# Gates turned on chip and stored as rows, in a gated mix of local attention and a Mish MLP

## The chip, the cores and the metric

The kernel runs on one core of a Trainium2 chip. The core has five engines with queues of their own: TensorE (PE in the profile) for matrix products, VectorE (DVE), ScalarE (ACT) and GpSimd (POOL) for everything between them, and SyncE (SP), which here only issues DMAs. Each works through its queue in order and waits on semaphores where it needs another's result. DMAs move data between the device's memory and the on-chip memory, which has 128 partitions. The metric is device time in microseconds; less is better.

## The reference

From one input x of 2048 rows and 640 columns two branches are computed: local attention with 32 heads, in which each position looks at 8 earlier positions, 2 apart, and an MLP with a Mish between its two products. A gate for each row mixes the two.

```python
def reference(A_x, A_wqkv, A_wo, B_x, B_w1, B_b1, B_w2, gate_w):
    ...
    x = A_x
    g = _sigmoid((x * gate_w).sum(-1, keepdims=True))
    a = _A_ref(x, A_wqkv, A_wo)
    b = _B_ref(x, B_w1, B_b1, B_w2)
    return g * a + (1 - g) * b
```

The change touches only how 1 - g, one number for each of the 2048 rows, gets from where it is computed to where it is used.

## The kernel before, in words

The rows are worked on in two halves (P = 0 and 1) of 1024, each as 8 slots of 128 rows. Products are made of float32 operands split into a high and a low part, three matmuls for one product (`mm3`, L457 to L462). The splitting is done by ACT (the high part, L410) and by DVE or POOL (the low part, L413); most loads land in `raw` or `hb` buffers and are split into `pair` buffers.

The work in order of TensorE's queue: for each half and each quarter of the heads a unit `qkv` (L634) makes queries, keys and values into PSUM banks `qb` and `sb`, from which ACT copies them (L624 to L630). Between the units lie the first product of the MLP (class `Quad`, L883, with sums and differences of blocks in the manner of Strassen) and Mish (ACT, L732 and L918), whose results go through `hb` buffers, are summed by `combined` (L804, run at L808) and stored to memory as `act` and `actt` blocks. Then come the second product of the MLP (`mlp2`, L1146) and the output product of the attention (`wo_part`, L1312). Attention itself (L497) runs on DVE: multiply (L517), sum (L520), softmax (L538 to L549), weigh (L558) and sum (L562), then a turn in blocks of 32 x 32 (L473) and four stores to `o`. Sums of the second-layer weights (`sums_of`, L983, with L998 and L1011) are made along the way and stored as `s`.

Each weight block of the first unit of a half (hq = 0) carries `gate_w` as extra columns. After a slot's product, ACT copies the one column of row sums into `zt[:, P, s]` (L630): 128 partitions by 8 slots. `make_gates` (L694) turns them into gates: ACT takes exp(-z) (L700), DVE adds 1, takes the reciprocal (g, used by the attention's softmax at L548) and computes 1 - g into `gc` (L696 to L698). One DMA (L702) then stores `gc` to `g_d[P]`, which lies in memory as 8 rows of 128 floats: slot by row. Element by element that is a transpose: consecutive floats of a partition of `gc` go to places 512 bytes apart. Much later `gates_in` (L1150) reads four rows at a time, broadcast over 128 partitions, into a buffer by which the MLP's results are multiplied (`gated`, L1173).

Nothing is placed in the engines' queues by hand. Each piece of work is a task (engine, estimated ns, function, what it comes after, buffers), and `Plan.run` (L105) simulates the engines with these estimates and emits the tasks in the order in which the simulation starts them. A task may be given to "ANY", and then goes to POOL, or to DVE when it is due. Among ready tasks the lowest rank goes first; `rank=2.0` for the store of the gates is behind nearly all other work of SP. The `size` of a DMA task sets how long the simulation lets it hold the wire: size/330 ns (L91), after all that is on the wire already (L200 to L203). So an estimate, a rank or a size changes the order of all later work. Buffers of a kind form a ring with a fixed number (6 `hb`, 8 `raw`, 24 `pair`), which are handed out in order.

Of the kernel before, what the change touches and what calls it, by code (L numbers as in the profile page):

```python
# [8 lines left out]
F32 = mybir.dt.float32  # L9
F32R = mybir.dt.float32r  # L10
AF = mybir.ActivationFunctionType
OP = mybir.AluOpType
# [54 lines left out]
class Plan:  # L67
# [21 lines left out]
    def add(self, eng, ns, fn, after=(), rank=0.0, take=(), hold=(), size=0, kind="", late=0):  # L89
        t = Task(eng, ns, fn, rank, size / 330.0)  # L90
        t.kind, t.late, t.near, t.patience = kind, late, self.NEAR, self.PATIENCE  # L91
        if eng == "POOL" and type(ns) is not tuple:
            t.ns = (ns, ns)
        for p in after:
            if p is not None:
                p.then.append(t)
                t.waits += 1
        t.take = list(take)
        t.hold = list(take) + [b for b in hold if b not in take]
        for b in t.hold:  # L100
            b.left += 1
        self.tasks.append(t)
        return t
# [136 lines left out]
def kernel(ctx: ExitStack, tc: tile.TileContext, x, wq, wo, w1, b1, w2, out):  # L240
    nc = tc.nc
    scale = DH ** -0.5
    V, G, A = nc.vector, nc.gpsimd, nc.scalar

    keep = ctx.enter_context(tc.tile_pool(name="keep", bufs=1))
# [93 lines left out]
    add = plan.add  # L339

    SOON, NEXT, LATER, LAST = 0.0, 1.0, 2.0, 3.0
# [5 lines left out]
    bound = keep.tile([1, HQ, 7], F32)  # L347
    zt = keep.tile([128, 2, 8], F32)
    gate = keep.tile([128, 2, 8], F32)
    gc = keep.tile([128, 2, 8], F32)  # L350
    hx = keep.tile([128, 2, 8, NQ, RQ], F32)

    keep.tile([128, 118], F32, name="gap")
# [11 lines left out]
    g_d = [dram.tile([8, 128], F32, name=f"g{P}") for P in range(2)]  # L365
# [5 lines left out]
    KV = [Late(lambda i=i: kvq[i][:, :15 * ROW].rearrange("p (s a f) -> p s a f", a=2, f=QF)) for i in range(3)]  # L371
# [27 lines left out]
    def consts_g():  # L399
        G.memset(KV[0][0:1, 0:7], 0.0)  # L400

        G.memset(bound, -BIG / scale)


    cg = [add("POOL", 2200, consts_g, rank=-1), add("DVE", 2200, lambda: V.memset(KV[1][0:1, 0:7], 0.0), rank=-3.0)]


    def split(raw, hi, lo, n, after, eng, hold, take=(), rank=SOON):
# [17 lines left out]
    def dma(out_ap, in_ap, after=(), rank=0.0, take=(), hold=(), size=262144, late=0):  # L426
        return add("SP", 450, lambda: nc.sync.dma_start(out_ap(), in_ap()), after, rank=rank, take=take, hold=hold, size=size, late=late)
# [206 lines left out]
    def qkv(u, P, hq, between={}):  # L634
# [51 lines left out]
        if not hq:  # L686
            gates[P] = [make_gates(P, [ev[i][2] for i in range(8)])]
# [3 lines left out]
    g_done = {}  # L691


    def make_gates(P, after):  # L694
        def run():
            V.tensor_scalar(zt[:, P], zt[:, P], 1e30, 1.0, op0=OP.min, op1=OP.add)  # L696
            V.reciprocal(gate[:, P], zt[:, P])
            V.tensor_scalar(gc[:, P], gate[:, P], -1.0, 1.0, op0=OP.mult, op1=OP.add)  # L698

        t = add("ACT", 200 + 2 * TABLE, lambda: A.activation(zt[:, P], zt[:, P], AF.Exp, scale=-1.0), after, rank=NEXT)  # L700
        t = add("DVE", 500, run, [t], rank=NEXT)
        g_done[P] = dma(lambda: g_d[P].rearrange("s p -> p s"), lambda: gc[:, P], [t], rank=2.0, size=400000)  # L702
        return t


# [572 lines left out]
    def rows(tb, kc):  # L1278
        return o_d[tb][kc * 128:(kc + 1) * 128]
# [419 lines left out]
```

## Time and profile before

| | us |
|---|---|
| median of 3 runs | 631.7 |
| lowest and highest run | 627.73, 631.99 |
| the profiled execution | 631.72 |
| its span, first to last instruction | 630.0 |

The table of the profile that says the most is the busy time of each engine in 40 equal slices of the span, in tenths, with TensorE's granted clock and the DMA engines' share:

```profile
PE   9999999999999999999999979999999999999997
PEld 7878888888888888888888758888888888888886
DVE  8699999999989999899999999999999989879955
ACT  6587637736476554624556365765845743556520
POOL 1487557657747553386564563586436750010000
PEclk9999999999999999999999989999999999999999
DMA  8668684577857799979987777668899664799613
```

A digit of 9 means 90% or more. Each slice is 15.75 us. A time in microseconds in the text below counts from the start of the span; a line such as L698 is that of the kernel before. Other views group instructions by line, follow the chain of waits back from the last instruction, or list engines in order of time, with the idle time before an instruction and what ended it in square brackets.

### The profile page before, as it was taken

The page shows a single profiled execution, that of the slowest core. Times are in us where ns is not written, and L with a number is a line of the kernel's source. Part 1 is how long each engine was busy: PE and PEld are TensorE (multiplying, and loading weights), DVE is VectorE, ACT ScalarE, POOL GpSimd, SP SyncE. Part 2 cuts the span into 40 slices and gives each one's busy share as a digit, 9 for nine tenths or more (in the row PEclk, how much of TensorE's full clock was granted, in tenths as well). Part 3 has the DMA queues.
Part 4 walks back from the last instruction along what each step waited for, and adds up shares of the span by engine and source line. Part 5 has one row for each costly group of instructions (what it writes and reads, how often), then busy time and mean ns, then how long its engine had stood idle before and what let it go on. Part 6 is the DMA issues. An engine that isn't in the chain of part 4 may idle for free.

```text
span 630.0 us, 9053 instructions
## 1 busy us (share of the span) xinstructions
PE 619.8 (98%) x2743; PEld 514.4 (82%) x2743; DVE 581.3 (92%) x547; ACT 349.9 (56%) x790; POOL 306.8 (49%) x281
## 2 busy tenths in 40 slices
PE   9999999999999999999999979999999999999997
PEld 7878888888888888888888758888888888888886
DVE  8699999999989999899999999999999989879955
ACT  6587637736476554624556365765845743556520
POOL 1487557657747553386564563586436750010000
PEclk9999999999999999999999989999999999999999
DMA  8668684577857799979987777668899664799613
GB/s 322 193 196 124 227 285 113 185 231 240 270 176 205 229 183 222 287 195 306 280 235 253 218 248 237 176 190 242 255 252 307 189 212 151 218 305 358 230 50 117
DMA packets 99552, 140.36 MB, mean 223 GB/s; under 512 B 13152, under 2 KB 53344, under 8 KB 99280
## 3 DMA queue, kind: packets, MB, share of 16 engines
q1 hardware_dynamic: 96144, 134.02, 68.0%
q0 software_dynamic: 3072, 5.51, 6.0%
q8 instruction: 21, 0.34, 0.2%
q10 hardware_dynamic: 288, 0.26, 0.1%
q14 instruction: 27, 0.22, 0.1%
HBM read 87.78 MB, written 51.00 MB: 220 GB/s over the span
## 4 chain that ended last, share of the span: by engine, by line
PE 74%; DVE 9%; DMA 8%; POOL 4%; issue 3%; ACT 2%; SPq 0%; DVEq 0%; POOLq 0%; ACTq 0%
PE qb L460 15%; PE qb L461 15%; PE qb L462 15%; PE sb L462 9%; PE sb L460 9%; PE sb L461 9%; DMA ot<-o 2%; DVE lg L520 2%; DVE pr L517 2%; POOL hb L808 2%; DVE pr L558 2%; DMA s<-raw 1%; DMA raw<-in_w 1%; POOL pair L413 1%; DMA ot<-ot 1%
## 5 line engine op out<-in xcount | busy, mean ns | idle before, releaser
L413 POOL TENSOR_TENSOR pair<-raw,pair 128x512 fp32r<-128x512 f32 (+3 forms) x132 | 163.6, 1274 | 102.5 <-ACT pair L410 50.7
L460 PE MATMUL qb<-pair 128*128 128x512 f32 (+1 forms) x467 | 181.8, 389 | 5.3 <-ACT hb L732 4.4
L461 PE MATMUL qb<-pair 128*128 128x512 f32 (+1 forms) x467 | 181.3, 388 | 0.0
L462 PE MATMUL qb<-pair 128*128 128x512 f32 (+1 forms) x467 | 181.3, 388 | 0.0
L410 ACT ACTIVATE pair<-raw 128x512 fp32r<-128x512 f32 (+3 forms) x223 | 129.5, 609 | 85.2 <-DMA raw<-actt 24.4
L460 PE MATMUL sb<-pair 128*128 128x512 f32 (+1 forms) x294 | 113.7, 387 | 0.0
L462 PE MATMUL sb<-pair 128*128 128x512 f32 (+1 forms) x294 | 113.7, 387 | 0.0
L461 PE MATMUL sb<-pair 128*128 128x512 f32 (+1 forms) x294 | 113.7, 387 | 0.0
L460 PEld LDWEIGHTS qb<-pair 128*128 128x128 f32 x467 | 87.9, 188 | 24.1 <-ACT hb L732 5.3
L462 PEld LDWEIGHTS qb<-pair 128*128 128x128 f32 x467 | 88.1, 189 | 17.4
L461 PEld LDWEIGHTS qb<-pair 128*128 128x128 f32 x467 | 88.1, 189 | 17.1
L558 DVE TENSOR_TENSOR pr<-kvq,pg 128x1280 f32<-128x1280 f32 x64 | 93.3, 1485 | 1.0
L517 DVE TENSOR_TENSOR pr<-kvq,qg 128x2560 f32<-128x2560 f32 x32 | 90.0, 2812 | 1.6
L520 DVE TENSOR_REDUCE lg<-pr 128x128 f32<-128x2560 f32 x32 | 90.2, 2818 | 0.8
L562 DVE TENSOR_REDUCE kvq<-pr 128x320 f32<-128x2560 f32 x32 | 90.2, 2817 | 0.8
L413 DVE TENSOR_TENSOR pair<-raw,pair 128x512 fp32r<-128x512 f32 (+3 forms) x91 | 65.5, 743 | 10.7 <-ACT pair L410 10.6
L462 PEld LDWEIGHTS sb<-pair 128*128 128x128 f32 x294 | 55.2, 188 | 11.3
L460 PEld LDWEIGHTS sb<-pair 128*128 128x128 f32 x294 | 55.2, 188 | 11.3
L461 PEld LDWEIGHTS sb<-pair 128*128 128x128 f32 x294 | 55.2, 188 | 11.2
L808 POOL TENSOR_TENSOR hb<-hb 128x512 f32<-128x512 f32 x41 | 53.5, 1313 | 18.1 <-DVE lg L539 4.7
L624 ACT ACTIVATE kvq<-qb 128x320 f32<-128x320 f32 x63 | 27.3, 434 | 57.2 <-PE qb L462 56.8
L410 ACT ACTIVATE pair<-hb 128x512 fp32r<-128x512 f32 (+3 forms) x62 | 36.6, 590 | 2.8 <-PE qb L462 1.4
(156 smaller groups left out, 735.0 us busy)
## 6 DMA issues: line engine op xcount, KB each, us to landing
actt<-hb SPq DMA_DIRECT2D x52, 256.0 KB, 3.3
raw<-in_w SPq DMA_DIRECT2D x40, 256.0 KB, 4.1
act<-hb SPq DMA_DIRECT2D x38, 256.0 KB, 3.0
raw<-actt SPq DMA_DIRECT2D x37, 256.0 KB, 4.1
raw<-in_wq SPq DMA_DIRECT2D x30, 248.0 KB, 3.5
raw<-act SPq DMA_DIRECT2D x29, 256.0 KB, 3.6
raw<-in_x SPq DMA_DIRECT2D x23, 256.0 KB, 3.5
o<-ot SPq DMA_DIRECT2D x64, 80.0 KB, 3.0
```

What stands on the lines that cost most here:

```text
L410: a = add("ACT", act_ns(n), lambda: A.activation(hi(), raw(), AF.Copy), after, rank=rank, take=take, hold=hold)
L413: return (V if e == "DVE" else G).tensor_tensor(lo(), raw(), hi().bitcast(F32), op=OP.subtract)
L460: nc.tensor.matmul(ps, ah, bh, start=first, stop=False, skip_group_check=more)
L461: nc.tensor.matmul(ps, ah, bl, start=False, stop=False, skip_group_check=more)
L462: nc.tensor.matmul(ps, al, bh, start=False, stop=last, skip_group_check=more)
L517: return V.tensor_tensor(pr, window(kv, s0, 0), qg[:, :, None, :].to_broadcast([128, 2, W, QF]), op=OP.mult)
L520: V.tensor_reduce(lg_w[:, s0:s0 + 2], pr.rearrange("p s w (h d) -> p s w h d", d=DH), op=OP.add, axis=AX.X)
L558: V.tensor_tensor(pairs[:, s].rearrange("p k i (h d) -> p k i h d", d=DH), vw, pg[:, s0 + s].rearrange("p (k i) h -> p k i h", i=2)[:, :, ...
L562: V.tensor_reduce(q[:, s0:s0 + 2], pairs.rearrange("p s k i f -> p s f k i"), op=OP.add, axis=AX.XY)
L624: a = add("ACT", 330, lambda: A.activation(kv[:, 7 + s], ps.t[:, QF:3 * QF].rearrange("p (a b) -> p a b", a=2), AF.Copy), [done] + before, ...
L808: return (V if e == "DVE" else G).tensor_tensor(t.t[:, i:i + n], a.t[:, j:j + n], b.t[:, k:k + n], op=op)
```

## The change

`gc` grows from 8 to 32 columns for each half and is filled with zeros at the start; the gates go into its first 8 columns. DVE turns each block of 32 partitions by 32 columns (`V.transpose`) into a second tile `gt`, in which slot s of a block of 32 rows now lies in partition 32 i + s. SP then issues four stores for each half, each of 8 partitions by 32 floats: 8 pieces of 128 bytes. The estimates that the planner is given change with it: 2200 to 2300 ns on POOL, 500 to 700 on DVE, 450 to 1800 on SP, and a size of 400000 to 65536.

```diff
-    gc = keep.tile([128, 2, 8], F32)
+    gc = keep.tile([128, 2, 32], F32)
+    gt = keep.tile([128, 2, 32], F32)
...
+        G.memset(gc, 0.0)
...
-    cg = [add("POOL", 2200, consts_g, rank=-1), add("DVE", 2200, lambda: V.memset(KV[1][0:1, 0:7], 0.0), rank=-3.0)]
+    cg = [add("POOL", 2300, consts_g, rank=-1), add("DVE", 2200, lambda: V.memset(KV[1][0:1, 0:7], 0.0), rank=-3.0)]
...
-            V.tensor_scalar(gc[:, P], gate[:, P], -1.0, 1.0, op0=OP.mult, op1=OP.add)
+            V.tensor_scalar(gc[:, P, :8], gate[:, P], -1.0, 1.0, op0=OP.mult, op1=OP.add)
+            V.transpose(gt[:, P], gc[:, P])
...
-        t = add("DVE", 500, run, [t], rank=NEXT)
-        g_done[P] = dma(lambda: g_d[P].rearrange("s p -> p s"), lambda: gc[:, P], [t], rank=2.0, size=400000)
+        t = add("DVE", 700, run, [t], rank=NEXT)
+
+        def rows():
+            for i in range(4):
+                nc.sync.dma_start(g_d[P][:, 32 * i:32 * (i + 1)], gt[32 * i:32 * i + 8, P])
+
+        g_done[P] = add("SP", 1800, rows, [t], rank=2.0, size=65536)
```

## The prediction

> **What bounds the kernel now.** I read the page first, then the busy time in equal stretches, then who waited for whom on PE.
>
> ```profile
> span 630.0 us, 9053 instructions
> PE 619.8 (98%) x2743; PEld 514.4 (82%) x2743; DVE 581.3 (92%) x547; ACT 349.9 (56%) x790; POOL 306.8 (49%) x281
> ```
> ```profile
> 40.00:50.00 10.00, 8.97 (x40) 7.11 (x39) 9.73 (x7) 8.64 (x18) 9.75 (x9) 1.00 0.82 187
> ...
> 360.00:370.00 10.00, 6.44 (x28) 4.75 (x26) 9.86 (x7) 7.87 (x16) 6.53 (x6) 1.00 0.72 236
> 370.00:380.00 10.00, 9.84 (x37) 8.13 (x38) 9.72 (x10) 4.22 (x14) 3.87 (x4) 0.83 0.95 285
> ```
> ```profile
> PE qb L460 <- ACT hb L732: 4.4, 2, 3.4
> PE qb L460 <- ACT hb L918: 0.8, 2, 0.5
> ```
>
> A stretch row gives the stretch, its length, then the busy time of PE, weight load, DVE, ACT and POOL, the granted clock, the DMA share and GB/s. PE is busy 619.8 of 630.0 us: a change can give back only PE's idle time and what slow clock follows it. Inside the work that is 1.0 us near 41, before any gate exists, and 4.2 us between 358 and 370 (in the waits, 3.4 of the 4.4 on L732 and the 0.8 on L918). The rest of the 10.2 us is the two ends of the program. So I look at the 358 to 370 stop and what feeds it.
>
> ```profile
> 358.41 0.69 ACT L918 ACTIVATE hb<-qb,bias 128x512 f32<-128x512 f32 x1 [10.00 <-DMA actt<-hb]
> ```
> ```profile
> 370.16 0.49 PE L460 MATMUL qb<-pair 128*128 128x496 f32 x1 [3.41 <-ACT hb L732]
> ```
> ```profile
> 42.55 0.23 PE qb L461
> ```
> ```profile
> 371.86 0.41 PE qb L460
> ...
> 374.34 0.41 PE qb L460
> 374.76 0.37 PE qb L461
> ```
>
> The last two fences are from the chain of waits: start, length, piece. The matmuls that follow the 3.41 us stop step at 0.41 us instead of 0.23 us, seven of them from 371.86 to 374.34 and one of 0.37: 7 x 0.18 + 0.14 = 1.4 us lost to the clock, which is the 0.83 in the 370 to 380 row. After the 1.03 us stop near 41 the step is 0.23 at once. The stop at 366 is therefore worth 3.41 + 1.4 = 4.8 us. ACT was late because a store had not freed its hb buffer; the store's source is written by DVE and POOL, and DVE is 98 to 99% busy through this stretch. DVE's lateness is what PE pays for here, so I ask where DVE lost time before 358.
>
> ```profile
> 247.26 0.42 DVE L538 TENSOR_REDUCE mx<-lg 128x32 f32<-128x256 f32 x1 [0.55 <-ACT lg L530]
> ```
> ```profile
> 267.68 0.42 DVE L998 TENSOR_TENSOR raw<-raw 128x256 f32<-128x256 f32 x1 [2.77 <-DMA raw<-in_w]
> ...
> 279.21 0.42 DVE L538 TENSOR_REDUCE mx<-lg 128x32 f32<-128x256 f32 x1 [1.07 <-ACT lg L530]
> ```
>
> Between the second gate (225 us) and 358, DVE waited 0.55 + 2.77 + 1.07 = 4.4 us, the largest part for a load.
>
> **What is removed.** The two old stores, in the view of their tile, and DMA traffic around them:
>
> ```profile
> L698 DVE TENSOR_SCALAR gc<-gate x2: 171/650/1128, 45.2 to 225.2; 128x8 f32<-128x8 f32 x2
> L427 SPq DMA_DIRECT2D g<-gc x2: 389/390/392, 46.3 to 228.8; - x2
> ```
> ```profile
> DMA to landing us min/median/max: 10.2/10.5/10.7
> ```
> ```profile
> 48.00:50.00 2.00, 2.00 (x11) 1.65 (x10) 1.91 (x2) 0.94 (x5) 2.00 (x2) 1.00 1.29 54
> ```
> ```profile
> 230.00:235.00 5.00, 5.00 (x24) 4.16 (x23) 4.86 (x6) 1.43 (x3) 3.91 (x5) 1.00 1.14 91
> 235.00:240.00 5.00, 5.00 (x25) 4.26 (x24) 4.86 (x4) 0.86 (x4) 4.49 (x4) 1.00 1.00 129
> ```
> ```profile
> DMA packets 99552, 140.36 MB, mean 223 GB/s; under 512 B 13152, under 2 KB 53344, under 8 KB 99280
> ```
> ```profile
> h<-pair SPq DMA_DIRECT2D x8, 32.0 KB, 2.8
> ```
>
> Each store moves 128 x 8 gates of 4 bytes, 4 KB, which by the shape of its destination are 1024 packets, and lands after about 10.45 us, where another small store lands after 2.8. Meanwhile the engines are full (shares of 1.29, 1.14, 1.00) and move almost nothing. From 230 to 240 they move about 110 GB/s against the mean of 223: 10 x 113/223 = 5 us of DMA work is pushed back; beside the first store the row from 48 to 50 shows 54 GB/s. An estimate per packet: (10.45 - 2.8) / (1024/16) = 0.12 us on each of 16 engines. The new stores have 4 x 8 = 32 packets of 128 bytes; at that price 0.24 us spread over 16, 3.8 us if one engine had them all. I take under 0.5 us.
>
> Who stood behind the second store:
>
> ```profile
> 228.31 9.38 DMA s<-raw
> ```
> ```profile
> 255.17 7.78 DMA ot<-o
> ```
> ```profile
> raw<-in_w SPq DMA_DIRECT2D x40, 256.0 KB, 4.1
> ot<-o SPq DMA_DIRECT2D x12, 256.0 KB, 4.0
> s<-raw SPq DMA_DIRECT2D x14, 64.0 KB, 3.8
> ```
>
> The store of sums issued at 228.31, just ahead of the gate store, took 9.38 us against a median of 3.8 and lies on the chain. The chain goes on through SP and a 7.78 us DMA at 255 (median 4.0), which finds the engines full with what was pushed back. The load that DVE waited for at 267.68 falls into the same crowd. I credit the change with that 2.77 us: between nothing (the crowd at 255 to 267 is also its own traffic) and 2.77 + 1.07 = 3.84 (the ACT wait at 279 starts with a load too). 2.77 is the wait that names a DMA directly. In the first half I credit nothing: PE has no wait between 43 and 358, and DVE's later waits there name ACT.
>
> **What is added.**
>
> ```profile
> L473 DVE STREAM_TRANSPOSE ot<-kvq 128x640 f32<-128x640 f32 x16 | 13.4, 840 | 0.2
> ...
> L473 DVE STREAM_TRANSPOSE pair<-hx 128x256 f32<-128x256 f32 x2 | 0.8, 421 | 0.0
> ...
> L402 POOL MEMSET bound<- 1x56 f32 x1 | 0.1, 135 | 0.0
> ```
> ```profile
> SPq L849 <- DMA act<-hb: 4.0, 1, 4.0
> ```
>
> A transpose costs (840 - 421)/384 = 1.09 ns per element, so 421 - 224 x 1.09 = 0.18 us for 32 columns. Upper bound: L698 itself took 1.128 us in one half and 0.171 in the other, the long one while POOL was at work, so 0.96 us more: 0.18 to 1.14 us; it cannot be below nothing, as the instruction is new. I take 0.18, since the hx transposes ran undisturbed. Behind it on DVE is the attention multiply (L517). Only the second half's is on the path to 358. The narrower write into gc's first 8 of 32 columns costs nothing new. The memset of gc is about 0.14 us (nearest row 0.135) on a POOL that starts idle; without that cover it would be 0.14.
>
> SP issues four stores for one: three more at 0.39 us, some 1.2 us in each half. Queued behind them are the four attention stores (o<-ot) and the weight loads. The cover is SP's own 4.0 us wait near 236 for a landing, itself prolonged by the old store; if that shrinks, the 1.2 us stands open. I take nothing, with 1.2 as the bound. The next reader, the broadcast of g, comes only at 333 us, so its latency is free.
>
> The Trainium skill, "DMA: Bandwidth & Descriptors", section "Rules for kernel authors", speaks against this change: it says to coalesce small transfers, as those under 64 KB mostly pay overhead. By that page's fixed cost of about 2 us per DMA, three more DMAs would be an estimated 6 us of latency in each half. The trace does not agree that joining pays here: the single store took 10.45 us to land, and nobody waits for it until 333. The same section of the Trainium skill says that a strided last dimension becomes one descriptor per element; the trace agrees in so far as 4 KB took 10.45 us.
>
> The edit also changes the numbers by which the planner deals out work: 500 to 700 ns on DVE, 450 to 1800 on SP, 2200 to 2300 on POOL, and the wire time (size/330) from 1212 to 199 ns. Every later order, and the choice of DVE or POOL for shared adds, may come out differently. The trace prices that from neither side; it is the main unknown.
>
> **Sum.** DVE reaches 358 earlier by 2.77 - 0.18 = 2.6 us; PE's 4.2 us of stops shrink by that to 1.6, none as long as 3.4, so the 1.4 us of slow clock goes too: 2.6 + 1.4 = 4.0 us. PE has no wait after 375, so it reaches the end. The profiled run took 631.72 us with a span of 630.0; 630.0 - 4.0 + 1.72 = **627.7 us**. The profiled run stands at the median (631.7); the runs before lie from 627.73 to 631.99.
>
> On the clock the Trainium skill, "TensorE: Matmul & The Clock Gate", Part 1, says that the clock falls after an idle window of about 3.4 us; the 3.41 us stop with its slow steps and the 1.03 us stop without agree.
>
> **Rivals.**
>
> Hidden (no change): the crowd at 255 to 267 persists, and the four stores cost SP 1.2 us. For it: those transfers run at full engines long after 240. Against: 5 us of pushed-back work fits the delay. Time 631.72 + 0.2 = 631.9. The Trainium skill's rule against small DMAs, named above, would end here too.
>
> Order (slower): the planner hands DVE more of the shared subtracts while P=1's quads run (230 to 375).
>
> ```profile
> L413 POOL TENSOR_TENSOR pair<-raw,pair 128x512 fp32r<-128x512 f32 (+3 forms) x132 | 163.6, 1274 | 102.5 <-ACT pair L410 50.7
> ```
> ```profile
> L413 DVE TENSOR_TENSOR pair<-raw,pair 128x512 fp32r<-128x512 f32 (+3 forms) x91 | 65.5, 743 | 10.7 <-ACT pair L410 10.6
> ```
>
> Each moved one adds 0.74 us to DVE, and DVE has only 4.4 us of slack before 358. Ten moved (of POOL's 132) are 7.4 us of PE stop: 639.1. It decides from 6.3/0.74, some nine. For it: PE's lead rests on an order with four small stops in 630 us, and a new order has far more room to be worse than better. Against: the planner still aims to keep PE fed, and its wire is now nearer to the truth.
>
> Full relief (faster by over 1%): all stops after 358 and the slow clock go, with the 1.03 us near 41 if the early order falls well: 4.2 + 1.4 + 1.0 = 6.6, so 625.1. It needs everything at once.
>
> **Numbers.** Forecast 0.40, hidden 0.22, order 0.30, full relief 0.08. One per cent is 6.3 us, about what a measurement of this kernel can tell from no change: below 625.4 is faster, above 638.0 slower. So faster 0.08, within 0.62 (forecast and hidden), slower 0.30. The range runs from 625.0, the most that PE's idle time allows, to 641.0, the order case with two or three more moved ones; the forecast's own range is 625.4 to 630.5.
>
> **What would show it.** Right: the gate stores land in under 4 us; GB/s from 48 to 56 and after the second gate stand near 223; the store of sums beside the second gate lands in about 4 us; DVE has no DMA wait of 2 us before 358; PE's stop on L732 is below 2 us and the clock there 1.00. Wrong: PE waits of over 3 us at new places, or many more L413 on DVE than 91, mean order; an unchanged 3.4 us stop with the DMA gap gone means hidden. The forecast falls if DVE's order before 358 is not the same in kind.

## The result: 624.2 us, and the profile after

| | us |
|---|---|
| before, median of 4 runs | 631.85 (627.73 to 632.33) |
| after, median of 4 runs | 624.16 (623.78 to 624.76) |
| ratio of after to before | 0.9885, 95% interval 0.9842 to 0.9928 |
| the profiled execution after | 624.5, span 622.7 |

The change made the kernel faster by 1.2%. Single runs of the kernel before differ by some 7 us: taken with the later experiments, 23 of them on one chip lay between 625.77 and 632.99. The forecast was 627.7, and the time is 0.8 us below the lower end of the range. What arrived is what the prediction called full relief and gave 0.08; but the 1.0 us near 41 us, which that case counted in, did not go.

The busy times on the page after, and PE's waits:

```profile
PE 616.9 (99%) x2743; PEld 513.3 (82%) x2743; DVE 578.8 (93%) x554; ACT 351.3 (56%) x790; POOL 299.6 (48%) x277
```
```profile
PE qb L462 <- ACT hb L740: 1.0, 1, 1.0
PE sb L394 <- PEq L1695: 0.8, 1, 0.8
```

L462 and L740 are L460 and L732 of before. The stops between 358 and 370 are gone. The same stretches as before:

```profile
230.00:235.00 5.00, 5.00 (x24) 4.16 (x23) 4.90 (x7) 2.53 (x7) 2.83 (x4) 1.00 0.87 213
235.00:240.00 5.00, 5.00 (x24) 4.26 (x24) 4.96 (x3) 2.10 (x7) 4.40 (x4) 1.00 1.03 277
...
360.00:370.00 10.00, 10.00 (x47) 8.45 (x46) 9.79 (x11) 4.54 (x11) 2.54 (x2) 1.00 0.87 283
370.00:380.00 10.00, 10.00 (x47) 8.55 (x46) 9.86 (x7) 5.22 (x19) 3.06 (x3) 1.00 0.80 216
```

From 230 to 240 the DMA engines move 213 and 277 GB/s where they moved 91 and 129, and PE is busy throughout 360 to 380 at the full clock. The count of DMA packets fell too:

```profile
DMA packets 97600, 140.36 MB, mean 225 GB/s; under 512 B 11200, under 2 KB 51392, under 8 KB 97328
```

Before there were 13152 packets under 512 bytes. 1952 are gone, close to the 2 x (1024 - 32) = 1984 that the prediction's count of packets gives. What was added:

```profile
L708 SPq DMA_DIRECT2D g<-gt x8: 280/297/330, 46.5 to 245.1; - x8
L701 DVE STREAM_TRANSPOSE gt<-gc x2: 211/212/213, 46.2 to 229.3; 128x32 f32<-128x32 f32 x2
```

A transpose takes 0.21 us, a store's issue 0.30. One shared subtract left POOL (131, formerly 132), not ten. Yet the plan did change: the second gates come out of DVE at 229.3 rather than 225.2, their stores are issued only at 245, and from 117 us on PE works through some of its units in another order. So two things changed at once, the store and the order, and the first experiments part them.

### The profile page after: what moved, and what is told of

Same layout as the page of the kernel before. It is cut to its first block, busy times and chain, and to the rows that moved or that the text cites. A ratio compares the mean times of both kernels' runs of the same rounds, so it can differ in the third digit from the quotient of the medians.

```text
span 622.7 us, 9060 instructions
## 1 busy us (share of the span) xinstructions
PE 616.9 (99%) x2743; PEld 513.3 (82%) x2743; DVE 578.8 (93%) x554; ACT 351.3 (56%) x790; POOL 299.6 (48%) x277
## 4 chain that ended last, share of the span: by engine, by line
PE 96%; ACT 1%; DVE 1%; issue 0%; POOL 0%; DVEq 0%
PE qb L462 20%; PE qb L463 20%; PE qb L464 20%; PE sb L462 11%; PE sb L463 11%; PE sb L464 11%; PE qb L620 1%; ACT pair L412 1%; DVE raw L816 1%; PE sb L394 1%; DVE pair L415 0%; PE qb L468 0%; PE sb L469 0%; PE sb L468 0%; PE qb L469 0%
## 5 line engine op out<-in xcount | busy, mean ns | idle before, releaser
L462 PE MATMUL qb<-pair 128*128 128x512 f32 (+1 forms) x467 | 180.7, 387 | 1.0 <-ACT hb L740 1.0
L462 PE MATMUL sb<-pair 128*128 128x512 f32 (+1 forms) x294 | 113.7, 387 | 0.0
L462 PEld LDWEIGHTS qb<-pair 128*128 128x128 f32 x467 | 87.7, 188 | 18.5 <-ACT hb L740 1.4
L415 DVE TENSOR_TENSOR pair<-raw,pair 128x512 fp32r<-128x512 f32 (+2 forms) x92 | 64.7, 727 | 5.1 <-ACT pair L412 5.0
L462 PEld LDWEIGHTS sb<-pair 128*128 128x128 f32 x294 | 55.2, 188 | 11.2
L816 POOL TENSOR_TENSOR hb<-hb 128x512 f32<-128x512 f32 x38 | 50.2, 1337 | 23.8 <-DVE ot L475 5.8
```

Source lines behind the costliest of these rows:

```text
L415: return (V if e == "DVE" else G).tensor_tensor(lo(), raw(), hi().bitcast(F32), op=OP.subtract)
L462: nc.tensor.matmul(ps, ah, bh, start=first, stop=False, skip_group_check=more)
L816: return (V if e == "DVE" else G).tensor_tensor(t.t[:, i:i + n], a.t[:, j:j + n], b.t[:, k:k + n], op=op)
```

## The experiments

My theory when they began: the old store's traffic made DVE late, and the new store alone gives the gain. The rival: the new order alone gives it.

**One part at a time.** The first kernel (E1 in the expectations) has the new store, with the planner's numbers of before, so that the queues of all engines hold the old order:

```diff
-        g_done[P] = add("SP", 1800, rows, [t], rank=2.0, size=65536)
+        g_done[P] = add("SP", 450, rows, [t], rank=2.0, size=400000)
```

(and 500 for 700 on DVE, 2200 for 2300 on POOL). What was expected:

> The changed store (transpose, four row stores, zeroed gc) in the old order: the planner keeps its old estimates (500, 450, 2200 ns, size 400000), so every engine's queue is that of before but for two transposes, one memset and six more stores. Theory 'store' (the 4-byte packets made DVE and POOL late, and PE paid for it between 358 and 376): all or nearly all of the gain is here, 624 to 626 us, no PE wait on L740 over 1 us after 50 us, clock 1.00. Theory 'order' (the new estimates dealt the work out better, the store itself was hidden): 631 to 633 us, with the 3.4 us wait still there.

The second (E2) has the new numbers, and so the new order, with the old store and no transpose:

```diff
-            V.transpose(gt[:, P], gc[:, P])
...
-            for i in range(4):
-                nc.sync.dma_start(g_d[P][:, 32 * i:32 * (i + 1)], gt[32 * i:32 * i + 8, P])
+            nc.sync.dma_start(g_d[P].rearrange("s p -> p s"), gc[:, P, :8])
```

> The old store of 4-byte packets in the new order: the planner has the new estimates (700, 1800, 2300 ns, size 65536), the queues are those of the changed kernel without the transposes and the memset, with one store for four. Theory 'store': the stop comes back in some place, 629 to 633 us. Theory 'order': 623.5 to 625.5 us. If both E1 and E2 gain, either cure is enough by itself: the stop has a margin, and both move it past.

| | median us (lowest to highest) | runs | ratio to before, 95% |
|---|---|---|---|
| new store, old order | 623.97 (623.43 to 625.52) | 4 | 0.9902, 0.9883 to 0.9921 |
| old store, new order | 624.19 (623.45 to 624.46) | 4 | 0.9899, 0.9885 to 0.9914 |
| both: the change | 624.16 (623.78 to 624.76) | 4 | 0.9885, 0.9842 to 0.9928 |

Each alone brings all of it, and together they bring no more. Both theories are half right. Here and below a ratio compares a kernel with runs of the kernel before that were taken with it. A difference in microseconds between two changed kernels can be one between chips, and is less sure: the kernel before had medians of 630.3 to 631.9 us in the four groups of runs.

With the new store in the old order, instructions can be laid side by side with before. First the transfers issued between 224 and 236 us, the median time to landing last in each row; before, then the new store:

```profile
raw<-in_w SPq DMA_DIRECT2D x3, 256.0 KB, 8.8
...
s<-raw SPq DMA_DIRECT2D x2, 64.0 KB, 9.5
```
```profile
raw<-in_w SPq DMA_DIRECT2D x3, 256.0 KB, 4.1
...
s<-raw SPq DMA_DIRECT2D x2, 64.0 KB, 2.7
```

These neighbours of the old store took some 9 us each, those of the new ones 2.7 to 4.1, with the same tiles from the same queue in the same order. DVE, in the new store's list in order of time (start, length), at the two instructions that stood at 267.68 and 279.21 before:

```profile
264.99 0.42 DVE L1006 TENSOR_TENSOR raw<-raw 128x256 f32<-128x256 f32 x1
...
275.36 0.41 DVE L540 TENSOR_REDUCE mx<-lg 128x32 f32<-128x256 f32 x1
```

Neither waits now. DVE is 2.69 us earlier at the first and 3.85 at the second. Then 2.35 us more appear where nothing waits for a DMA: 0.54 right behind the second, where a sum (L808) takes 1.14 us instead of 1.39 and a subtract (L539) 0.68 instead of 0.96, and 1.81 in one multiply. The multiply before, then with the new store:

```profile
319.05 2.81 POOL L413 TENSOR_TENSOR pair<-raw,pair 128x512 fp32r<-128x512 f32 x2
319.39 2.53 DVE L548 TENSOR_TENSOR sm<-sm,gate 128x32 f32<-128x32 f32 x1
```
```profile
312.85 2.81 POOL L415 TENSOR_TENSOR pair<-raw,pair 128x512 fp32r<-128x512 f32 x2
...
315.00 0.72 DVE L550 TENSOR_TENSOR sm<-sm,gate 128x32 f32<-128x32 f32 x1
```
```profile
L548 DVE TENSOR_TENSOR sm<-sm,gate x16: 185/192/2534, 63.8 to 501.4; 128x32 f32<-128x32 f32 x16
```

The last row is the line's 16 durations before (lowest, median, highest in ns): a 0.19 us multiply took 2.53, and ends at 321.92, 0.06 us after POOL's pair of subtracts (321.86). With the new store it starts later within the same pair, takes 0.72 us, and ends at 315.72, 0.06 after it (315.66). DVE's multiply waited for POOL, and 1.81 us less of it with the new store. The Trainium skill, "SBUF — State Buffer", section "SBUF: two separate sides", says that a VectorE operation with two inputs on chip and a GpSimd operation that reads there shut each other out for a whole instruction; the two ends agree, and these rows add that the multiply was shut out over two of POOL's instructions in a row. At 344.68 before and 338.48 with the new store stand the same instructions:

```profile
344.68 2.82 DVE L520 TENSOR_REDUCE lg<-pr 128x128 f32<-128x2560 f32 x1
```
```profile
338.48 2.82 DVE L522 TENSOR_REDUCE lg<-pr 128x128 f32<-128x2560 f32 x1
```

So DVE comes 6.2 us earlier to the place where PE depends on it. The chain of waits before shows how PE depends on it at the long stop: from a subtract of DVE through POOL's sums and ACT's Mish to the matmul at 370.16.

```profile
362.82 0.43 DVE lg L539
...
366.89 2.51 POOL hb L808 x2
...
369.42 0.70 ACT hb L732
```

Now PE. Its matmuls start 0.15 us apart in the two traces up to 358, and 7.21 apart from 400 to the end: all of the gain between them, 7.06 us, arises where the stops were (these two executions took 631.72 and 624.26 us). Before, then, with the new store, the matmuls that stand at 359.15 and (quoted in the prediction) 370.16 before:

```profile
358.23 0.39 PE L462 MATMUL qb<-pair 128*128 128x512 f32 x1
359.15 0.50 PE L460 MATMUL qb<-pair 128*128 128x512 f32 x1 [0.53 <-ACT hb L918]
359.48 0.39 PE L461 MATMUL qb<-pair 128*128 128x512 f32 x1
...
366.37 0.38 PE L462 MATMUL qb<-pair 128*128 128x496 f32 x1
```
```profile
358.31 0.39 PE L462 MATMUL qb<-pair 128*128 128x512 f32 x1
...
365.01 0.38 PE L462 MATMUL qb<-pair 128*128 128x496 f32 x1
```

Between the two rows the distance to before grows from 0.84 to 5.15 us. The idle time in brackets is not the price of a stop. It is counted from the modelled end of a matmul (0.39 us long), while matmuls follow each other every 0.23. From start to start the first stop is 0.92 instead of 0.23, so 0.69 for 0.53 of idle, and the first step after it is 0.33 (359.15 to 359.48), 0.10 more. The long one is 370.16 - 366.37 = 3.79 instead of 0.22, so 3.57 for 3.41, and 0.11 more. With the third stop, 0.58, the three come to 5.05 us, not 4.2. Eight slow steps between 371.66 and 374.96 took 3.30 us instead of 1.76, which with the step before them is 1.6. That leaves 0.4 of the 7.06: after the stop, 15 of these matmuls take 3.35 us instead of 3.30 up to 391 and a little beyond. I don't know why.

With the old store in the new order, the harm is still there and PE hardly feels it. The stretches in which the store now lands, and the one where PE stopped before; then DVE's wait for the load:

```profile
245.00:250.00 5.00, 5.00 (x25) 4.26 (x24) 4.93 (x3) 3.39 (x6) 4.21 (x4) 1.00 1.11 129
250.00:255.00 5.00, 5.00 (x25) 4.26 (x24) 4.97 (x4) 1.28 (x6) 0.00 (x0) 1.00 0.98 89
360.00:370.00 10.00, 9.86 (x45) 8.01 (x44) 9.83 (x12) 5.80 (x11) 3.44 (x3) 1.00 0.64 207
```
```profile
DVE raw L1006 <- DMA raw<-in_w: 2.8, 1, 2.8
```

In the changed kernel the first two moved 199 and 213 GB/s. PE has one wait that the changed kernel does not have, of 0.3 us. The 2.8 us load wait is back, and DVE is later than in the changed kernel, in the same order; the first row is of the old store, the second of the change:

```profile
301.77 1.48 DVE L560 TENSOR_TENSOR pr<-kvq,pg 128x1280 f32<-128x1280 f32 x1
```
```profile
298.17 1.48 DVE L560 TENSOR_TENSOR pr<-kvq,pg 128x1280 f32<-128x1280 f32 x1
```

3.6 us of lateness cost no time that the medians show: the new order has that much room on DVE.

**Which of the two stores.** The old order, with the new store in one half alone:

```diff
+            if P == 1:
+                V.transpose(gt[:, P], gc[:, P])
...
+            if P != 1:
+                return nc.sync.dma_start(g_d[P].rearrange("s p -> p s"), gc[:, P, :8])
```

> Old order; the second half's gates (near 225 us) go by the new way, the first half's (near 45 us) by the old store. My step credited the second store alone: then this equals E1 within 1 us. If the first store's block also carries over through DVE, it is 1 us or more above E1.

And with 0 for 1 in both conditions:

> Old order; the first half's gates go by the new way, the second half's by the old store. By my step: no gain, 631 to 633 us. If the first block is what makes DVE late, it is 1 us or more below that.

| | median us (lowest to highest) | runs | ratio to before, 95% |
|---|---|---|---|
| second half only | 624.95 (624.48 to 630.66) | 9 | 0.9933, 0.9901 to 0.9965 |
| first half only | 629.45 (628.19 to 631.88) | 10 | 0.9995, 0.9977 to 1.0013 |

The second half's store is the one that counts. Alone it comes out 0.98 us above E1, just within the expected microsecond. The first half's alone came out below the 631 to 633 us that were expected for no gain, but so did the kernel before on that chip (630.34); the ratio is the measure, and it shows no gain. PE's longest wait is then that of before:

```profile
PE qb L462 <- ACT hb L743: 4.4, 2, 3.4
```

Two of the nine runs of the second half's store lie above 630; whether the first half's store adds room that makes such runs rarer can't be told from so few.

**How late may DVE be?** The changed store with the old order, and a gap on DVE behind the second gates: fills of a tile that nothing reads, 157 ns each.

```diff
+            for _ in range(16 if P else 0):
+                V.memset(gap, 0.0)
```

> E1 (new store, old order) with DVE held up after the second half's gates by 16 memsets of an unused tile, about 3 us by the slope of L405 (1925 ns for 2240 columns) and some fixed part. Theory 'DVE's lateness is what PE pays': before, DVE was 6.2 us later than E1 at 322 us and PE lost 5 us to stops and 1.5 us to the clock, so the old order bears about 1.2 us; 3 us of lateness give a stop of some 1.8 us with no slow clock: 625 to 627 us. Rival 'a DMA, not DVE, holds the hb buffers': no change from 624.0.

With 32 fills in the old order (E6):

> The same with 32 memsets, about 6 us. Theory 'DVE's lateness': the stop of before comes back with the new store in place: 4.8 us of stops, and the slow clock if one of them is over about 3.4 us: 628 to 632 us, PE waiting for L740. Rival 'a DMA': 624.

With 32 fills in the changed kernel, the new order:

> The changed kernel with the same 32 memsets after the second half's gates. If the new order only shifted the meeting points a little, it stops as E6 does: 628 to 632 us. If the new order bears more lateness of DVE (E2 was 3.6 us later than the changed kernel at 302 us and PE did not wait), it stays at 624 to 626 us.

| | DVE later from 265 us on, us | median us (lowest to highest), 10 runs | ratio to before, 95% |
|---|---|---|---|
| old order, 16 fills | 3.8 to 5.3 | 629.66 (624.22 to 631.64) | 0.9982, 0.9954 to 1.0011 |
| old order, 32 fills | 7.6 to 9.3 | 633.03 (630.42 to 634.8) | 1.0047, 1.0023 to 1.0072 |
| new order, 32 fills | 6.1 to 7.0 | 628.41 (626.91 to 632.13) | 0.9983, 0.9958 to 1.0009 |

PE's waits of the three, in this order:

```profile
PE qb L462 <- ACT hb L742: 4.4, 2, 3.4
```
```profile
PE qb L462 <- ACT hb L742: 3.5, 2, 2.5
PE qb L462 <- ACT hx L630: 3.2, 1, 3.2
```
```profile
PE qb L462 <- ACT hb L928: 2.1, 1, 2.1
```

Of the 4.4 on L742, 1.0 is the wait near 41; the same holds for the 3.5. No store of 4-byte elements is here, and yet the first kernel stops PE for 3.4 us at the old place: lateness of DVE is enough by itself. Both kernels of the old order came out slower than was expected (625 to 627 and 628 to 632). The lateness was larger than the gap: the multiply beside POOL's pair of subtracts took 2.22 and 2.47 us again, ending 0.06 us after the pair in both, and DVE is 5.3 and 9.3 us late from there on. The 5.3 us cost 629.66 - 623.97 = 5.7, slow clock included, so the room there is about 1.6 us (an estimate: 5.3 us later, less the 3.7 of the long stop). Two of its ten runs took 624.22 and 626.40, too little for such a stop and its slow clock; why is not known. Twice the gap costs 9.1 us, but not at the old place alone: 3.2 us of the waiting, on hx (L630), lie near 257, where before has no stop, and the trace is of the slowest of the ten runs. The new order bears 3.6 (above). With 32 fills it loses 4.2 (628.41 - 624.16), at the lower end of what was expected if it stopped like E6, so it has more room than the old order, but not for a gap of that size.

**Which of the planner's numbers.** Old store, with 1800 on SP alone, then with 700 on DVE alone, all other numbers as before:

```diff
+        g_done[P] = add("SP", 1800, rows, [t], rank=2.0, size=400000)
```

> Old store, old estimates but one: the planner takes the store's issue on SP for 1800 ns instead of 450 (size stays 400000). The order then changes only from the second half's gates on. If this estimate carries E2's gain: 623.5 to 625.5 us. If not: 629 to 632 us, with PE's stop on L740 near 360 to 370.

```diff
+        t = add("DVE", 700, run, [t], rank=NEXT)
```

> Old store, old estimates but one: DVE's gate step is taken for 700 ns instead of 500. The order changes from the first half's gates on. If E2's gain is in the order that this gives: 623.5 to 625.5 us. If any other order is as likely to stop PE as that of before: 628 us or more, the stop at another place.

SP's number alone gave 626.93 us (624.27 to 629.65, 10 runs; ratio 0.996, 0.9934 to 0.9986), DVE's alone 627.73 (626.25 to 629.0, 10 runs; 0.9966, 0.9941 to 0.9991). The largest wait of PE in each that is not in the changed kernel:

```profile
PE qb L462 <- ACT hx L630: 3.1, 1, 3.1
```
```profile
PE qb L462 <- ACT hb L926: 1.0, 1, 1.0
```

Neither came out as expected: the first lies between its two ranges, the second just below its upper one. The trace of the first is of the slowest of its ten runs (629.65), and its fastest (624.27) can't hold such a stop. Each is a third order, with stops at other places than before; neither brings all that both numbers together bring. What the last number does, the size of 65536, was not run alone. Which moved unit gives the new order its room stays open.

**The wait near 41.** ACT turns the first gates between two table loads, and the first Mish stands behind them. I let the planner hold the first half's exp back by 5000 ns:

```diff
-        t = add("ACT", 200 + 2 * TABLE, lambda: A.activation(zt[:, P], zt[:, P], AF.Exp, scale=-1.0), after, rank=NEXT)
+        t = add("ACT", 200 + 2 * TABLE, lambda: A.activation(zt[:, P], zt[:, P], AF.Exp, scale=-1.0), after, rank=NEXT, late=0 if P else 5000)
```

> The changed kernel with the first half's gate exponential (ACT, with its table load) planned 5 us later, so that it no longer stands ahead of the Mish for which PE waits 1.0 us near 41 us. If that table load is what delays the Mish: PE's wait near 41 goes and the time is 622.8 to 623.8 us. The planner's order changes for all later work, so a new stop elsewhere would show as 624 or more.

It gave 629.76 us (628.7 to 631.14, 10 runs; ratio 0.9997, 0.9974 to 1.002), 5.6 us above the changed kernel: the plan came out anew, and PE's largest wait now begins near 43 us, with slow steps behind it.

```profile
PE sb L462 <- ACT sb L920: 2.5, 2, 2.1
```

So the last kernel leaves the plan as the changed kernel has it and moves only the instructions: the first half's exp is issued right behind the first softmax's exp, which has its table loaded already, DVE's part ahead of that softmax's first sum, and the stores ahead of the first attention stores.

```diff
+    def off(e, fn, P):
+        return fn if P else lambda: put_off[e].append(fn)
...
+    def now_do(e):
+        while put_off[e]:
+            put_off[e].pop(0)()
...
-            e = add("ACT", 360 + 2 * TABLE, lambda: A.activation(lg[:, h], lg[:, h], AF.Exp, scale=scale), [t], rank=-1, late=1500)
+            e = add("ACT", 360 + 2 * TABLE, lambda: (A.activation(lg[:, h], lg[:, h], AF.Exp, scale=scale), now_do("ACT"))[0], [t], rank=-1, late=1500)
...
-        t = add("ACT", 200 + 2 * TABLE, lambda: A.activation(zt[:, P], zt[:, P], AF.Exp, scale=-1.0), after, rank=NEXT)
-        t = add("DVE", 700, run, [t], rank=NEXT)
+        t = add("ACT", 200 + 2 * TABLE, off("ACT", lambda: A.activation(zt[:, P], zt[:, P], AF.Exp, scale=-1.0), P), after, rank=NEXT)
+        t = add("DVE", 700, off("DVE", run, P), [t], rank=NEXT)
```

> The changed kernel, planned as it is, but the first half's gate work is emitted later: the exponential right behind the first softmax's exponential (ACT, two table loads fewer), the DVE steps ahead of the first sum of shares, the stores ahead of the first attention stores. All else keeps its order. If the table load in front of the Mish is why PE waits 1.0 us near 41 us, that wait goes: 622.7 to 623.4 us, ahead of the changed kernel's 624.2. If PE then waits for something right behind (the Mish's own end), less than 0.4 us is gained.

It gave 623.31 us (623.06 to 623.98, 6 runs; ratio to before 0.9902, 0.9876 to 0.9929), with a span of 621.4 where the changed kernel's was 622.7. ACT's list in order of time, of the changed kernel and then of this one:

```profile
38.06 1.28 ACT L703 ACT_TABLE_LOAD   x1
...
39.92 1.28 ACT L740 ACT_TABLE_LOAD   x1
41.21 1.27 ACT L740 ACTIVATE hb<-qb,bias 128x512 f32<-128x512 f32 x2
```
```profile
38.84 1.25 ACT L749 ACTIVATE hb<-qb,bias 128x512 f32<-128x512 f32 x2
```

Mish starts at 38.84 rather than 41.21, and PE has no wait left but the 0.8 us at its start. This is the fastest kernel here, 0.85 us below the changed one by the medians. The two were not timed side by side and their runs overlap (623.06 to 623.98 and 623.78 to 624.76), so the trace carries this rather than the times.

## Why the prediction was wrong

**Where the time was** was right: PE is the bound, its stops between 358 and 370 and the slow clock behind them were all that the change could give back, and all that it gave back. The wait near 41 us, before any gate, stayed in the changed kernel.

**How the old store reached it** was right as well: full engines that move little, neighbours landing after 9 us instead of 3 to 4, the load that DVE waits for at 267, DVE late, ACT late, PE stopped. At the long stop the way from DVE to ACT leads through POOL's sums; a store that holds ACT's buffer, which the prediction read at 358, belongs to the first and short stop. Crediting only the second half was right (0.9995 for the first half's store alone).

**The step that failed** is the first term of the sum, "DVE reaches 358 earlier by 2.77 - 0.18 = 2.6 us; PE's 4.2 us of stops shrink by that to 1.6". With the order kept, the load wait gave 2.69, so that row was read rightly. But DVE came 6.2 us earlier: the wait for ACT at 279 went too (I had 3.84 as the upper end and measured 3.85), and 2.35 us more came from DVE instructions that took less time, 1.81 of it from a multiply that waited for less of POOL's two subtracts. Those 2.35 were nowhere in my bounds, though the 1.128 us beside 0.171 of L698, which I used for the transpose, showed such a meeting. 6.2 is more than the 5.05 us of stops; the difference, 1.1, is the room that the old order has on DVE, and the gap experiment gave about 1.6 for it. By the same account 3.85 alone would have left about 5.05 - 3.85 = 1.2 us of stops: an estimate, not run.

**The prices of the stops** were the second error: 4.2 us of idle and 1.4 of slow clock in place of 5.05, 1.6 and 0.4, so 5.6 for 7.06. For that reason the lower end, "the most that PE's idle time allows", lay above what was possible: 625.0 counted idle time as the profile gives it, from the modelled end of a matmul.

**The order** was "the main unknown", and I let it count on one side only. It could cost: the three other plans (626.93, 627.73, 629.76) each have new stops in their traces and lie 2.8 to 5.6 us above the change, though not by the ten moved subtracts that I priced, for POOL keeps 128 to 133 of them. None of them is slower than the kernel before (ratios 0.996, 0.9966, 0.9997), so the slower rival, at 639, did not show in any order that was run. The change's own order, which comes with its new numbers, turned out to be a second cure, which alone gives 0.9899. So the change would have come out the same if the store had brought nothing. That the two don't add is no puzzle: a stop that is gone can't be removed again.

**What was added** cost about what was said: 0.21 us for a transpose (0.18 said), 0.30 for an issue (0.39). The four issues did not delay the neighbours' landing (2.7 to 4.1 us). For these stores the Trainium skill's advice to coalesce small transfers ("DMA: Bandwidth & Descriptors", "Rules for kernel authors"), which spoke against the change, is not borne out: four stores in place of one, in the same order, brought 0.9902. The same section's rule on strided last dimensions, which the prediction cites, is the one that decides here. That the new stores land in under 4 us could not be read: the trace has no landing for them in the changed kernel.

## What to carry to other kernels

A store that scatters 4-byte elements was dear here for its neighbours and not for itself: look at what was issued just before and after it, and at the GB/s while the engines are full. Price a stop of PE from start to start of its matmuls, with the slow steps behind it, and price lateness on the feeding engine by what it does to the stop, which here was nothing until the room was used up, and then the rest of the lateness and the slow steps (5.3 us late cost 5.7, with 1.6 of room). Where a planner orders the work, run the new numbers with the old code and the new code with the old numbers before giving the credit to either.

## What the runs showed of the hardware

Stops shorter than 3.4 us can be followed by slow clock too. The 2.5 us stop of the old order with 32 fills was (matmuls of 496 columns step at 0.41 us, not 0.22), and so was the 2.1 us stop of the exp held back (512 columns, 0.43, not 0.23); the 2.1 us stop of the new order with 32 fills was not (0.22). Stretches just behind each, the granted clock third from last:

```profile
374.00:376.00 2.00, 2.00 (x8) 1.60 (x7) 2.00 (x1) 1.78 (x5) 2.00 (x2) 0.66 0.91 298
```
```profile
46.00:48.00 2.00, 2.00 (x6) 1.56 (x5) 1.90 (x6) 0.99 (x5) 0.00 (x0) 0.50 1.00 169
```
```profile
365.00:367.00 2.00, 1.61 (x7) 1.40 (x8) 2.00 (x3) 1.71 (x4) 0.68 (x1) 1.00 0.69 202
```

The Trainium skill, "TensorE: Matmul & The Clock Gate", Part 1, gives an idle window of about 3.4 us. The first two stops don't fit that as a threshold on the length of a stop; the measurement decides, and what sets one 2.1 us stop apart from another was not found.
